# Two banks instead of one for the value products of every attention phase

## The chip, the cores and the metric

The kernel runs on one core of a Trainium2 chip. The metric is the time of one execution in device microseconds; lower is better. The engines are named as in the profile: PE (matmuls), PEld (its weight loads), DVE (VectorE), ACT (ScalarE), POOL (GpSimd) and SP (the queue that issues DMAs). A bank is one of the eight 128 x 512 fp32 areas of PSUM, into which PE writes.

## The reference: what is computed

For 2048 tokens of width 512 the kernel mixes an attention block and a token-mixing MLP by a gate per token:

```python
q, k, v = (x @ wqkv) in 32 heads of width 16
p = softmax(q k^T * 16 ** -0.5)
a = (p v) @ wo
u = gelu(layernorm(x)^T @ w1 + b1); b = (u @ w2 + b2)^T
out = g * a + (1 - g) * b          # g = sigmoid(sum(x * gate_w))
```

All of it is float32. The softmax needs exp of 32 x 2048 x 2048 scores, which is what the long middle part of the kernel does.

## The kernel before, in words

**The stages.** Up to about 284 us the kernel projects v, k and half of q and runs the first MLP layer. Then come 128 *phases* of attention, p = 0 to 127, that end near 1231 us, and last the output projection's second half. Dense work (the second MLP layer, the other half of q, the first half of the output projection) is laid beside the attention, a few matmuls with each score matmul. The change touches the phases alone.

**A phase.** 32 groups of four phases (p = 4 * grp + ph) each treat two heads and half of the queries. In a phase PE makes 16 *units* of scores, n = 0 to 15, each a 128 x 512 bank (L1067); most units have a dense matmul beside them (L1076) on the other 64 rows of the array. The work is in an order written out by hand, and every engine runs its instructions in program order.

- Units 1, 3, 5, 9, 14 and 15 (`EVAC`) are copied from their bank to SBUF by DVE (L1089), and ACT then takes exp of all six in one instruction of 3072 columns (L1102), here called the *long exp*.
- Units 0, 2, 4, 6, 7 and 8 (`SINGLE`) go through exp on ACT one by one (L1093); units 10 with 11 and 12 with 13 go in pairs (L1031).
- Then PE makes the *value products* (L963), exp(scores) times v and a column of ones. In a phase these are 12 products of the units *held* from the phase before (1 with 3, 5 with 9, 14 with 15: their long exp has run since) and 20 of the phase's own units, the *turns* (0 with 2, 4 with 6, 7 with 8 and the two pairs). In the trace each product is two matmul records: 24 and 40 records.
- DVE adds the bank of products to the group's sum `ot` in SBUF (L985). Its next instruction is the copy of unit 1 of the next phase.

Two kinds of phases matter below. With **14** dense matmuls beside the units (second MLP layer), all own turn products are of one half of the sum's columns, and PE ends the units in the order 14, 15. With **12** (`late_query`, phases p = 8m + 6 and 8m + 7 for m = 0 to 7; output projection, p = 112 to 127) units 12 to 15 mix the two heads, so the turns cover one half of the columns and 64 rows of the other half, and PE ends with 15, 14.

**The banks.** Seven banks are dealt out anew in each phase by `shares`: unit n < 7 writes bank `share[n]`, units 7 to 13 write `share[0]` to `share[6]` again, unit 14 `share[0]` and unit 15 `share[2]`. `av`, the bank of the products, is `share[1]`, which unit 8 leaves. The bank that holds the last products is given to `shares` as `spare` and is used last in the next phase, by unit 6. In ph = 0 the held units belong to the group before, so there the held products go to `av` and the turns to a second bank, `share[3]`, which unit 10 leaves; DVE then adds twice. In the other three phases of a group held products and turns add up in `av`, and DVE adds all 512 columns once:

```python
if ph == 0:
    if held:
        apply_v(av, grp - 1, held, final=True)
        spare = share[3]
        av = twos[spare]
    apply_v(av, grp, turns)
elif p < LAST:
    apply_v(av, grp, held + turns, await_loads=ph == PHASES - 1)
```

`apply_v` issues the products and then the adds. It makes one add of 128 x 512 if all four pairs of head and query half are met, and else one of 128 x 256 for each head whose two query halves are met and one of 64 x 256 for a lone one. Between the copies of units 14 and 15 and these adds DVE runs what else is due in the phase: a tiny memset `mark` (L1111), splits of weights (L67, with POOL doing L68), results of the dense work (L542, L616 to L630, L816) and steps of the output projection (L755, L756, L1119).

Of the kernel before, what the change touches and what calls it, by code (L numbers as in the profile page):

```python
# [60 lines left out]
def gated_mix(ctx: ExitStack, tc: tile.TileContext, a_x, a_wqkv, a_wo, b_w1, b_b1, b_w2, b_b2, gate_w, out):  # L61
# [116 lines left out]
    with tc.tile_pool(name="vp", bufs=1, side="right") as pool:  # L178
# [15 lines left out]
        turns = {}  # L194
# [386 lines left out]
    PHASES, NSC, BANKS = 4, 16, 7  # L581
    LAST = NG * PHASES - 1
# [220 lines left out]
    def o_matmuls(half, t, n, m):  # L803

        for i in range(n, m):
            k, j = divmod(i, 3)
            hi, lo = o_parts[half, t % 8, k]
            a, b = ((hi, wo[0]), (hi, wo[1]), (lo, wo[0]))[j]
            yield a, b[: a.shape[0], k, :]
# [114 lines left out]
    def shares(n):  # L924

        for one in range(0, BANKS, 2):
            lows = [k for k in range(one)][::2] + [k for k in range(one + 1, BANKS)][::2]
            for third in lows:
                if n in (third, third + 1):
                    first, second = (low for low in lows if low != third)  # L930
                    return [first, first + 1, one, second, second + 1, 2 * third + 1 - n, n]
# [7 lines left out]
    def column_halves(x):  # L939
        x = x.rearrange("p (i m c) -> p m i c", i=2, m=2)  # L940
        return x[:, 0], x[:, 1]

    def store(g, ot):
        half, p = divmod(g, NP)
        k, p = divmod(p, 4)
        for j in range(4):
            rows, cols = slice(32 * j, 32 * j + VC), slice(j * QC, (j + 1) * QC)
            dst = o_d[half][k][2 * p * DH : 2 * (p + 1) * DH, cols].rearrange("(i r) n -> r i n", i=2)
            nc.sync.dma_start(dst, ot[rows][:DH].rearrange("r (i n) -> r i n", i=2))
            dst = r_d[half][k][None, 2 * p : 2 * (p + 1), cols]  # L950
            nc.sync.dma_start(dst, ot[rows][DH:].rearrange("r (i n) -> r i n", i=2))

    def apply_v(av, grp, pairs, final=False, await_loads=False, between=None):

        for n, pair in enumerate(pairs):
            if between and n == len(pairs) - 2:
                between()
            for i, c, qb, pt in sorted(pair, key=lambda u: u[2]):
                for h in range(2):
                    j = 2 * qb + h  # L960
                    b, r = divmod(grp % NP * 2 + i, BH)
                    v_at = (c * BH + r) * VC
                    mm = nc.tensor.matmul(  # L963
                        av[32 * j : 32 * (j + 1), i * QC : (i + 1) * QC],
                        vb[b][:, v_at : v_at + 32],
                        pt[:, h * QC : (h + 1) * QC],
                        start=n == 0,
                        stop=n == len(pairs) - 1,
                    )
                    if await_loads and n and landed:  # L970
                        tc.add_manual_dep(mm.ins, landed.pop(0).ins.name, SYNC, reason=AHEAD_OF_USE)
        ot = sums[grp]
        met = {(i, qb) for pair in pairs for i, _, qb, _ in pair}
        every, cols, rows = slice(0, P), [slice(n * QC, (n + 1) * QC) for n in range(2)], [slice(0, HALF), slice(HALF, P)]
        if grp == NG - 1 and final:
            assert len(met) == 4
            parts = list(zip(column_halves(ot), column_halves(av)))
        elif len(met) == 4:
            parts = [(ot, av)]
        else:  # L980
            at = [(every, cols[i]) for i in range(2) if {(i, 0), (i, 1)} <= met]
            at += [(rows[qb], cols[i]) for i, qb in sorted(met) if (i, 1 - qb) not in met]
            parts = [(ot[r, c], av[r, c]) for r, c in at]
        for x, y in parts:
            latest["add"] = nc.vector.tensor_tensor(x, y, x, ALU.add)  # L985
        if final and grp < NG - 1:
            store(grp, sums.pop(grp))

    engines = {getattr(mybir.EngineType, name) for name in ("PE", "Activation", "DVE", "Pool", "SP")}
    with tc.manual_schedule(engines=engines):  # L990
        held, fence, turn, spare = [], None, 0, 0
        landed.clear()

        for p in range(LAST + 1):
            grp, ph = divmod(p, PHASES)
# [42 lines left out]
            share = shares(spare)  # L1038
# [3 lines left out]
            for n in in_turn:  # L1042
# [7 lines left out]
                else:  # L1050
                    if n == TWO[0][0]:
# [4 lines left out]
                        for low in range(BANKS):  # L1056
                            if low == share[1]:
                                av = psum.tile([P, NB], F32, name="av")
# [61 lines left out]

            turns, now_held = ([tuple(units[n] for n in pair) for pair in pairs] for pairs in (TURNS, HELD))
            spare = share[1]
            if ph == 0:
                if held:
                    apply_v(av, grp - 1, held, final=True)
                    spare = share[3]
                    av = twos[spare]
                apply_v(av, grp, turns)
            elif p < LAST:
                apply_v(av, grp, held + turns, await_loads=ph == PHASES - 1)  # L1130
            else:
                ot = sums[grp]
                nc.vector.tensor_scalar_max(ot, ot, least[0])
                first_out = ps_dn.tile([P, D], F32, name="dn")

                def meanwhile():
                    for i, (a, b) in enumerate(o_matmuls(1, NH, 0, 3)):
                        nc.tensor.matmul(first_out, a, b, start=i == 0, stop=False)

                apply_v(av, grp, held + turns + now_held, final=True, between=meanwhile)  # L1140
                last_ot = ot
            pool.__exit__(None, None, None)
            held = now_held
# [86 lines left out]
    with tc.If(far_off != 0):  # L1230
        with (
# [6 lines left out]
            for b in range(ND):  # L1238
                with tc.For_i(0, P // DH, 1) as hi:
# [11 lines left out]
                    for t in range(NS):  # L1251
# [7 lines left out]
                        p = pool.tile([P, S], F32, name="p", bufs=1)  # L1259
# [51 lines left out]
```

## Time and profile before

| what | value |
|---|---|
| median of 3 runs | 1265.47 us (1265.09 to 1265.52) |
| the profiled execution | 1265.31 us |
| its span, first to last instruction | 1263.5 us |
| mean granted TensorE clock | 0.999 |
| busy: PE, ACT, DVE, POOL | 1254.8, 1069.0, 856.7, 198.6 us |
| one phase, from end to end of the long exp | 7.41 us |

A row of a timeline gives the start in the span, the time from the first start to the last end of equal neighbours, the engine, the line, the operation, output <- inputs, the shapes and the count; in brackets stands how long the engine was idle before, and what ended that. Instructions of one engine can overlap in such rows, since the next one starts before the one before has written its last element. A row of groups gives the busy time, the mean duration in ns of one, and the idle time before.

### The profile page before, as it was taken

How to read it: one execution, taken by the hardware profiler on the slowest of the kernel's cores; microseconds unless marked ns; L12 is line 12 of the kernel's file. 1: busy time of each engine (PE TensorE's matmuls, PEld its weight loads, DVE VectorE, ACT ScalarE, POOL GpSimd, SP SyncE). 2: the span in 40 equal slices, each digit the busy share in tenths (PEclk: the TensorE clock that was granted, in tenths of full speed). 3: DMA queues.
4: the chain of work that ended last, by engine and by line, in shares of the span. 5: the costliest groups of instructions: out<-in, count | busy, mean ns of one | idle time of the engine just before them, and what ended most of it. 6: DMA issues, size and time to landing. Idle time of an engine off the chain costs nothing.

```text
span 1263.5 us, 32833 instructions
## 1 busy us (share of the span) xinstructions
PE 1254.8 (99%) x13342; PEld 829.2 (66%) x13342; DVE 856.7 (68%) x1562; ACT 1069.0 (85%) x1405; POOL 198.6 (16%) x316
## 2 busy tenths in 40 slices
PE   9999999999999999999999999999999999999998
PEld 7888888875666666666666666666666666666656
DVE  5675453178767676767677677776777677678883
ACT  4443343269999999999999999999999999999990
POOL 0220444461010101010110101111111111000000
PEclk9999999999999999999999999999999999999999
DMA  4799443244744444544344433444543443366611
GB/s 134 251 340 329 143 122 106 81 127 110 214 121 104 90 102 85 158 86 97 77 105 94 99 90 83 91 87 81 113 101 73 90 100 60 56 166 175 151 60 70
DMA packets 100556, 152.32 MB, mean 121 GB/s; under 512 B 17109, under 2 KB 56171, under 8 KB 96300
## 3 DMA queue, kind: packets, MB, share of 16 engines
q1 hardware_dynamic: 99820, 149.08, 46.0%
q8 instruction: 107, 1.75, 0.6%
q10 hardware_dynamic: 576, 1.05, 0.2%
q14 instruction: 53, 0.43, 0.1%
HBM read 105.39 MB, written 44.68 MB: 119 GB/s over the span
## 4 chain that ended last, share of the span: by engine, by line
PE 96%; DVE 2%; ACT 1%; issue 0%; DVEq 0%
PE av L963 31%; PE s L1067 21%; PE acc L424 12%; PE t L1067 9%; PE acc L75 8%; PE t L963 5%; PE dn L1076 3%; PE u L1067 3%; PE pa L1162 2%; DVE pe L1089 1%; PE acc L199 1%; PE acc L268 0%; DVE ot L985 0%; PE acc L245 0%; ACT p L1093 0%; ACT pe L1102 0%
## 5 line engine op out<-in xcount | busy, mean ns | idle before, releaser
L1093 ACT ACTIVATE p<-s 128x512 f32<-128x512 f32 x768 | 411.9, 789 | 0.1
L1102 ACT ACTIVATE pe<-pe 128x3072 f32<-128x3072 f32 x129 | 380.9, 2954 | 0.0
L1067 PE MATMUL s<-qs,ks 64*128 64x512 f32 x1280 | 329.8, 400 | 0.6 <-ACT p L1093 0.6
L1089 DVE COPY pe<-s 128x512 f32<-128x512 f32 x512 | 323.6, 685 | 5.5 <-PE s L1067 1.5
L1067 PEld LDWEIGHTS s<-qs,ks 64*128 64x128 f32 x1280 | 225.7, 184 | 92.7 <-issue 52.3
L1031 ACT ACTIVATE p<-t 128x1024 f32<-128x1024 f32 x256 | 278.7, 1267 | 0.0
L963 PE MATMUL av<-p,v 128*32 128x256 f32 x3880 | 227.2, 379 | 0.0
L1089 DVE COPY pe<-u 128x512 f32<-128x512 f32 x256 | 164.8, 685 | 67.1 <-PE u L1067 67.1
L963 PE MATMUL av<-pe,v 128*32 128x256 f32 x3072 | 192.5, 383 | 0.0
L985 DVE TENSOR_TENSOR ot<-av,ot 128x512 f32<-128x512 f32 (+2 forms) x160 | 93.0, 582 | 140.9 <-PE av L963 139.6
L68 POOL TENSOR_TENSOR w_lo<-w_raw,w_hi 128x512 fp32r<-128x512 f32 (+1 forms) x128 | 153.0, 1202 | 196.8 <-ACT w_hi L67 99.9
L1076 PE MATMUL dn<-u_lo,w_hi 64*128 64x512 f32 x448 | 181.0, 404 | 0.0
L1076 PE MATMUL dn<-u_hi,w_hi 64*128 64x512 f32 x448 | 180.7, 403 | 0.0
L963 PEld LDWEIGHTS av<-p,v 128*32 128x32 f32 x3880 | 126.0, 110 | 83.3 <-ACT p L1093 0.2
L1076 PE MATMUL dn<-u_hi,w_lo 64*128 64x512 f32 x448 | 180.6, 403 | 0.0
L1067 PE MATMUL t<-qs,ks 64*128 64x512 f32 x512 | 142.5, 413 | 0.0
L963 PEld LDWEIGHTS av<-pe,v 128*32 128x32 f32 x3072 | 86.8, 109 | 80.7 <-ACT p L1093 35.7
L1080 POOL MEMSET token<- 1x1 f32 x128 | 11.3, 88 | 742.7 <-PE dn L1076 679.4
L67 ACT CAST w_hi<-w_raw 128x512 fp32r<-128x512 f32 (+1 forms) x67 | 38.0, 569 | 82.7 <-PE acc L424 63.1
L1067 PEld LDWEIGHTS t<-qs,ks 64*128 64x128 f32 x512 | 73.2, 184 | 50.8 <-ACT p L1093 48.6
L424 PE MATMUL acc<-h_hi,w_hi 128*128 128x512 f32 x224 | 87.9, 392 | 0.0
L424 PE MATMUL acc<-h_hi,w_lo 128*128 128x512 f32 x224 | 87.9, 392 | 0.0
(171 smaller groups left out, 1615.8 us busy)
## 6 DMA issues: line engine op xcount, KB each, us to landing
w_raw<-in_B_w_dram SPq DMA_DIRECT2D x96, 256.0 KB
ks<-kp SPq DMA_DIRECT2D x192, 128.0 KB
qs<-qp SPq DMA_DIRECT2D x256, 64.0 KB
kp<-pc SPq DMA_DIRECT2D x16, 512.0 KB
qp<-pc SPq DMA_DIRECT2D x8, 768.0 KB
qp<-row SPq DMA_DIRECT2D x24, 256.0 KB
v<-v SPq DMA_DIRECT2D x4, 1088.0 KB
x<-in_A_x_dram SPq DMA_DIRECT2D x16, 256.0 KB
```

Source lines behind the costliest of these rows:

```text
L67: copy(hi, src)
L68: return sub(lo, src, hi.bitcast(F32), ALU.subtract)
L75: nc.tensor.matmul(ps, a, b, start=start and n == 0, stop=stop and n == last)
L424: nc.tensor.matmul(p, a, b, start=first and k == 0, stop=last and k == 2)
L963: mm = nc.tensor.matmul(av[32 * j : 32 * (j + 1), i * QC : (i + 1) * QC], vb[b][:, v_at : v_at + 32], pt[:, h * QC : (h + 1) * QC], start= ...
L985: latest["add"] = nc.vector.tensor_tensor(x, y, x, ALU.add)
L1031: pairs_done.append(nc.scalar.activation(pt, twos[low, low + 1], AF.Exp, scale=SCALE))
L1067: nc.tensor.matmul(s, kt[grp][rows_i, c * P : (c + 1) * P], qt[grp][rows_i, qb * NB : (qb + 1) * NB], start=True, stop=True,)
L1076: mm = nc.tensor.matmul(ps, a[half], b[half], start=begin and not second, stop=last and bool(second))
L1089: nc.vector.tensor_copy(pt, s)
L1093: one = nc.scalar.activation(pt, s, AF.Exp, scale=SCALE)
L1102: done = nc.scalar.activation(x, x, AF.Exp, scale=SCALE)
```

## The change

In every phase except the last the held products now go to `av`, with adds of their own, and the turns to a second bank, which is now `share[0]` (unit 14 leaves it) and no longer `share[3]`, in ph = 0 too. Nothing else is edited.

```diff
-            if ph == 0:
+            if p < LAST:
                 if held:
-                    apply_v(av, grp - 1, held, final=True)
-                    spare = share[3]
+                    apply_v(av, grp - (ph == 0), held, final=ph == 0)
+                    spare = share[0]
                     av = twos[spare]
-                apply_v(av, grp, turns)
-            elif p < LAST:
-                apply_v(av, grp, held + turns, await_loads=ph == PHASES - 1)
+                apply_v(av, grp, turns, await_loads=ph == PHASES - 1)
```

On DVE, in a phase of 14 dense matmuls near the start of the attention (p = 1), `u_2800` being the new bank of the turns, the end of the phase and the start of the next read so before (-) and now (+):

```order
-L985 TENSOR_TENSOR ot<-av,ot 128x512
+L985 TENSOR_TENSOR ot<-av,ot 128x256
+L985 TENSOR_TENSOR ot<-av,ot 64x256
+L985 TENSOR_TENSOR ot<-u_2800,ot 128x256
```

One add has become three, of which the last alone needs the end of the products.

On DVE in a phase of 12 dense matmuls (p = 115, output projection), from the copies of units 15 and 14 to the copy of unit 1 of the next phase, before:

```order
L1089 COPY pe<-u_16963 128x512
L1089 COPY pe<-u_16964 128x512
L816 SCALAR_TENSOR_TENSOR row<-dn,g,row 128x512
L1111 MEMSET mark 1x1
L1119 TENSOR_TENSOR o_sum<-e_16664,o_sum 128x512
L1119 CAST e_16664<-o_sum 128x512
L1119 TENSOR_TENSOR e_16664<-o_sum,e_16664 128x512
L985 TENSOR_TENSOR ot<-av,ot 128x512
L1089 COPY pe<-s_17052 128x512
```

and now, where `u_17154` is the bank that unit 14 left:

```order
L1089 COPY pe<-u_17153 128x512
L1089 COPY pe<-u_17154 128x512
L816 SCALAR_TENSOR_TENSOR row<-dn,g,row 128x512
L1111 MEMSET mark 1x1
L1119 TENSOR_TENSOR o_sum<-e_16848,o_sum 128x512
L1119 CAST e_16848<-o_sum 128x512
L1119 TENSOR_TENSOR e_16848<-o_sum,e_16848 128x512
L985 TENSOR_TENSOR ot<-av,ot 128x256
L985 TENSOR_TENSOR ot<-av,ot 64x256
L985 TENSOR_TENSOR ot<-u_17154,ot 128x256
L985 TENSOR_TENSOR ot<-u_17154,ot 64x256
L1089 COPY pe<-s_17245 128x512
```

One add has become four, two of them after the end of the products, and the copy of unit 1 stands behind all four.

On PE, at the same kind of place (p = 117), the semaphores awaited in brackets, before:

```order
L1067 MATMUL u_17227<-qs_2583,ks_2582 128x512 [waits Activation_49]
L963 MATMUL av<-pe,v_114 32x256 [waits Activation_49]
L963 MATMUL av<-pe,v_114 32x256 x11
L963 MATMUL av<-p_17185,v_114 32x256 x2
L963 MATMUL av<-p_17192,v_114 32x256 x2
```

and now:

```order
L1067 MATMUL u_17420<-qs_2583,ks_2582 128x512 [waits Activation_49]
L963 MATMUL av<-pe,v_114 32x256 [waits Activation_49]
L963 MATMUL av<-pe,v_114 32x256 x11
L963 MATMUL u_17420<-p_17378,v_114 32x256 [waits DVE_49]
L963 MATMUL u_17420<-p_17378,v_114 32x256
L963 MATMUL u_17420<-p_17385,v_114 32x256 x2
```

The products and their order are the same, but the first product of the turns now waits for DVE, which has to copy unit 14 out of the bank first.

## The prediction

> **What bounds the kernel now.** I began with the page's first part, whose busy shares mislead here.
>
> ```profile
> span 1263.5 us, 32833 instructions
> PE 1254.8 (99%) x13342; PEld 829.2 (66%) x13342; DVE 856.7 (68%) x1562; ACT 1069.0 (85%) x1405; POOL 198.6 (16%) x316
> ```
>
> PE looks full and ACT looks free for 15% of the span. The groups by shape say otherwise:
>
> ```profile
> L1093 ACT ACTIVATE p<-s 128x512 f32<-128x512 f32 x768 | 411.9, 789 | 0.1
> L1102 ACT ACTIVATE pe<-pe 128x3072 f32<-128x3072 f32 x127 | 377.9, 2976 | 0.0
> L1031 ACT ACTIVATE p<-t 128x1024 f32<-128x1024 f32 x256 | 278.7, 1267 | 0.0
> ```
>
> Before its exps, the whole work of the phases, ACT idles 0.1 us in all; its free 15% lie outside the attention. How tight it runs, the timeline of ACT in two ordinary phases shows (p = 56 and 57):
>
> ```profile
> 699.24 3.00 ACT L1102 ACTIVATE pe<-pe 128x3072 f32<-128x3072 f32 x1
> 701.94 3.24 ACT L1093 ACTIVATE p<-s 128x512 f32<-128x512 f32 x6
> 704.81 2.19 ACT L1031 ACTIVATE p<-t 128x1024 f32<-128x1024 f32 x2
> 706.65 3.00 ACT L1102 ACTIVATE pe<-pe 128x3072 f32<-128x3072 f32 x1
> ```
>
> The ends are 702.24, 705.18, 707.00 and 709.65. They follow each other with no hole, 2.94 + 1.82 + 2.65 = 7.41 us per phase, and the starts lie before the ends of the instruction ahead. So ACT is saturated and has a little queue of begun work. How large it is, a place shows where ACT had to wait (p = 116 and 117):
>
> ```profile
> 1144.56 2.86 ACT L1102 ACTIVATE pe<-pe 128x3072 f32<-128x3072 f32 x1
> 1147.23 3.12 ACT L1093 ACTIVATE p<-s 128x512 f32<-128x512 f32 x6
> ...
> 1152.22 2.77 ACT L1102 ACTIVATE pe<-pe 128x3072 f32<-128x3072 f32 x1
> 1154.89 3.02 ACT L1093 ACTIVATE p<-s 128x512 f32<-128x512 f32 x6
> ```
>
> After the wait six single exps take 3.02 us instead of 3.24: about **0.22 us** of queue had been used up. From end to end of the long exp this phase took 1154.99 - 1147.42 = 7.57, so 0.15 or 0.16 us was lost. The kernel is bound by ACT. An edit on DVE cannot make a phase shorter than 7.41 us; it can only make ACT wait.
>
> **Is DVE's last add on the path?** The split form exists already, in ph = 0. Here are p = 56 (split) and p = 57 (one add):
>
> ```profile
> 701.60 0.42 DVE L985 TENSOR_TENSOR ot<-t,ot 128x256 f32<-128x256 f32 x1 [1.04 <-issue]
> 701.74 0.40 PE L1067 MATMUL s<-qs,ks 64*128 64x512 f32 x1
> 702.17 2.52 DVE L1089 COPY pe<-s 128x512 f32<-128x512 f32 x4 [0.15 <-PE dn L1076]
> ...
> 708.82 0.50 PE L1067 MATMUL s<-qs,ks 64*128 64x512 f32 x1
> 708.96 0.69 DVE L985 TENSOR_TENSOR ot<-av,ot 128x512 f32<-128x512 f32 x1 [1.85 <-PE av L963]
> 709.16 0.39 PE L1067 MATMUL s<-qs,ks 64*128 64x512 f32 x1
> 709.59 2.52 DVE L1089 COPY pe<-s 128x512 f32<-128x512 f32 x4
> ```
>
> Unit 1 is the matmul at 701.74 and at 709.16 (708.82 is unit 0). It ends at 702.14 and at 709.55, and its copy starts 0.03 and 0.04 us later, in both forms. The shorter add leaves DVE idle for 0.15 us and gains nothing. That settles the phases with 14 dense matmuls.
>
> **The change, part by part.** Prices of the adds, from the groups:
>
> ```profile
> L985 DVE TENSOR_TENSOR ot<-av,ot 128x512 f32<-128x512 f32 x95 | 65.6, 690 | 134.4 <-PE av L963 134.1
> L985 DVE TENSOR_TENSOR ot<-av,ot 128x256 f32<-128x256 f32 x34 | 14.2, 421 | 5.5 <-PE av L963 5.5
> L985 DVE TENSOR_TENSOR ot<-av,ot 64x256 f32<-64x256 f32 x31 | 13.3, 428 | 1.0
> ```
>
> The 95 adds of 512 columns are the 95 phases that change their form. 68 of them have 14 dense matmuls and get 421 + 428 + 421 ns for 690, 27 (16 late-query, 11 output projection) get a further 428. That is 68 x 0.58 + 27 x 1.01 = 67 us more of DVE, on an engine with 134.4 us of idle time just before these adds. What counts is where it falls. Back to back such adds are about 0.45 us apart, so a pair holds DVE for 0.90 us.
>
> *1. The 68 phases with 14 dense matmuls: 0, but for four.* The held pair needs 0.90 us of DVE's wait for the products (1.85 us above), and the last add is shorter by 0.2. Where there was no idle time before the add, the next copy comes 0.90 - 0.20 = 0.7 us late. There are four such places, p = 3, 83, 89 and 101; the first, the third and the last:
>
> ```profile
> 308.38 0.69 DVE L985 TENSOR_TENSOR ot<-av,ot 128x512 f32<-128x512 f32 x1
> ...
> 944.47 1.80 DVE L1119 TENSOR_TENSOR row<-v,row 128x512 f32<-128x512 f32 x1
> 946.40 0.69 DVE L985 TENSOR_TENSOR ot<-av,ot 128x512 f32<-128x512 f32 x1
> ...
> 1035.42 0.69 DVE L985 TENSOR_TENSOR ot<-av,ot 128x512 f32<-128x512 f32 x1
> ```
>
> No row of an add shows idle time in brackets. In p = 89 (the rows at 944.47 and 946.40) the add follows 946.40 - 946.27 = 0.13 us behind other work, and I take the same for p = 101, so there the copy comes 0.57 us late, and in p = 3 and 83, with nothing between, 0.7. ACT's queue takes 0.22, and about 0.1 is slack between copy and exp (see 2): 0.3 us each, **+1.2 us**.
>
> *2. The output projection, p = 113 to 126.* Here "half of the columns" does not hold: the turns need two adds after the last product. The form is in the trace already, in ph = 0 (p = 116):
>
> ```profile
> 1128.42 1.29 DVE L1089 COPY pe<-u 128x512 f32<-128x512 f32 x2 [0.59 <-PE u L1067]
> ...
> 1131.65 0.55 DVE L756 RECIPROCAL inv<-inv 128x64 f32<-128x64 f32 x1
> ...
> 1146.86 0.86 DVE L985 TENSOR_TENSOR ot<-t,ot 128x256 f32<-128x256 f32 x2 [0.99 <-issue]
> 1147.76 2.48 DVE L1089 COPY pe<-s 128x512 f32<-128x512 f32 x4
> 1150.83 1.29 DVE L1089 COPY pe<-u 128x512 f32<-128x512 f32 x2 [0.59 <-PE u L1067]
> ...
> 1153.29 0.69 DVE L1119 TENSOR_TENSOR e<-o_sum,e 128x512 fp32r<-128x512 f32 x1
> ```
>
> ```profile
> 1144.39 2.34 PE L963 MATMUL t<-p,v 128*32 128x256 f32 x40
> ...
> 1146.67 0.49 PE L1067 MATMUL s<-qs,ks 64*128 64x512 f32 x1
> ...
> 1152.05 2.34 PE L963 MATMUL av<-p,v 128*32 128x256 f32 x40
> ```
>
> Unit 0 starts at 1146.67, and unit 1 is copied 1.09 us later, where it is 709.59 - 708.82 = 0.77 in an ordinary phase: 0.32 late. That is the wait that cost ACT 0.16 with 0.10 of queue left (3.12 - 3.02), so some 0.06 to 0.1 is slack on the way. In ph = 0 it comes once in four phases and ACT recovers; now every phase has it. And a second thing closes the circle: the turns' first product waits until DVE has copied unit 14, the last copy. From copy to copy a phase is now: four copies and units 15 and 14 with theirs, 1147.76 to 1152.12, 4.36; PE's start after a copy, some 0.06; the 40 records to unit 0, 2.28; to the first add 0.19; the pair, 0.90. Together 7.79, **0.37** over ACT's 7.42. This is the floor, in p = 113, 116, 120 and 124.
>
> Where DVE has much else to do, its own row of work is longer: 4.36, then the other work D, then both pairs, 1.80. In p = 114 D reaches from 1129.71 to 1132.20 (2.4 after overlap), in p = 117 from 1152.12 to 1153.98, 1.86. So 8.57 and 8.02, **1.15** and **0.60** over. By the timeline p = 114, 115, 118 and 122 are of the first kind, p = 117, 119, 121, 123, 125 and 126 of the second. Sum: 4 x 0.37 + 4 x 1.15 + 6 x 0.60 = 9.7; about 0.5 of that is lost already (after the four ph = 0 phases, at about the 0.16 seen here or less). **+9.2 us.**
>
> *3. The eight pairs of late-query phases.* After p = 8m + 6 there are two adds, 0.90 for 0.63, and the turns start some 0.06 later: 0.33 late. In the next phase (p = 63, before):
>
> ```profile
> 746.66 2.52 DVE L1089 COPY pe<-s 128x512 f32<-128x512 f32 x4
> ...
> 749.78 1.29 DVE L1089 COPY pe<-u 128x512 f32<-128x512 f32 x2
> ...
> 752.24 0.68 DVE L623 TENSOR_REDUCE z<-dn 128x1 f32<-128x512 f32 x1
> ```
>
> From 746.66 DVE works to 752.92 and then has 1.80 us of adds: 8.06 from copy to copy, 0.64 over. Of 0.97 in all, 0.22 goes into ACT's queue and 0.1 into slack: 0.65 per pair, **+5.2 us**, and six ordinary phases lie between pairs for the queue to fill again.
>
> **The sum.** 1.2 + 9.2 + 5.2 = 15.6 us on the profiled execution's 1265.3 (span 1263.5 and 1.8 around it; the median of 1265.47 is the same within 0.2): **1280.9 us**.
>
> No row shows PE's own wait for the copy of unit 14. Its price lies between 0, if the 12 held products take as long as the copies, and 0.2 us, about half a matmul's 0.40, in each of 27 phases; I took 0.06 after the copies' end. They end at 1152.12 and the turns began at 1152.05, so the wait itself moves PE by 0.13.
>
> **Rivals.**
>
> *The held adds are held up by POOL* (slower still). In 16 phases POOL splits two weights, some 2 us right when the held adds are due. If these had to wait for POOL, they would end about 0.7 us later: 16 x 0.4 = 6.5 more, 1287. POOL's row at the place above:
>
> ```profile
> 944.43 2.43 POOL L68 TENSOR_TENSOR w_lo<-w_raw,w_hi 128x512 fp32r<-128x512 f32 x2 [1.76 <-DVE w_hi L67]
> ```
>
> The DVE product of two SBUF tiles at 944.47 took 1.80 us beside it, but the add of `av` at 946.40 took its usual 0.69 although POOL was at work until 946.86. So I give this 6%. The Trainium skill ("SBUF — State Buffer", "Who interferes with whom") says that a DVE instruction with two SBUF inputs contends with a GpSimd instruction that reads SBUF, and one with at most one SBUF input outside the two-port modes does not; these adds read `av` from PSUM, so by that rule the 6.5 us would not come, and the rows agree.
>
> *Not slower: ACT's queue takes it all.* One mechanism, at ACT's wait for the copies of units 14 and 15: a lateness under 0.22 us, with quiet phases after it in which the queue fills, costs nothing. For it: the 0.32 us in p = 117 cost only 0.16. It decides if the second add costs DVE little (the one add of 512 columns took 0.69, the pair 0.86 and a start); if each late phase stayed under that point, 2 and 3 would shrink to their full-DVE phases' queue and the time be 1265 to 1268. Against it: the pair comes 0.32 late where it can be seen, and from p = 113 no quiet phase follows. 7%.
>
> *Faster: the last add was what the next phase waited for.* Then each of the 68 phases would gain what DVE now idles after the short add, 0.15 us: 10.2 us, and with nothing of 1 to 3 the time would be 1255. It needs unit 1's copy to start late in the one-add form, and it starts 0.04 us after unit 1; and ACT's ends leave no hole. 3%.
>
> *Milder: only the phases whose DVE is full pay.* If the loop of 7.79 ran at 7.5 in fact, 1280.9 less 4 x 0.3 in 2 and less 8 x 0.3 in 3, and 0.2 less in each longer phase: 1275. This belongs to the forecast's range.
>
> **Numbers.** The forecast with its milder form has 84%, the rivals 6, 7 and 3. Range 1272 to 1288: from a loss of 6.7 us, where the copies' slack is twice what I took and the DVE-full phases overlap more, to POOL's rival. A measurement of this kernel can tell about 0.2%, 2.5 us, from no change. Faster by more 0.03, within 0.06, slower 0.91.
>
> **What would show it.** In the profile after: ACT's long exps still 7.41 us apart in phases of 14 dense matmuls; two more idle stretches on ACT after each late-query pair, some 0.65 us together; 7.8 to 8.6 us per phase from p = 113; DVE's adds of 64x256 more numerous than 150; PE's units 15 and 14 waiting for DVE copies. The forecast is wrong if late phases stay at 7.4, or if ordinary ones move.

## The result and the profile after

| | before | changed |
|---|---|---|
| median of 3 runs | 1265.47 us | 1276.86 us (1276.43 to 1278.03) |
| ratio | | 1.009, interval 1.0077 to 1.0104 |
| profiled execution, its span | 1265.31, 1263.5 us | 1276.43, 1274.7 us |
| from the end of the first to that of the last long exp | 936.15 us | 947.01 us |

The change made the kernel 11.4 us slower; 15.4 had been forecast, within a range that reaches from 6.5 to 22.5 over before. The long exps hold 10.86 us of it. What lies ahead of the first long exp, 0.36 us here, is chance, since up to there the two programs are the same: in the kernels below that exp ends anywhere from 285.5 to 286.3 us. Behind the last long exp the change shows once more, since the end of p = 126 is late too. ACT's first work after the attention, before and now:

```profile
1234.69 0.41 ACT L1180 CAST e<-o_sum 128x256 fp32r<-128x256 f32 x1 [5.24 <-DVE o_sum L1179]
```

```profile
1246.59 0.41 ACT L1178 CAST e<-o_sum 128x256 fp32r<-128x256 f32 x1 [5.77 <-DVE o_sum L1177]
```

This cast starts 12.74 us after the end of the last long exp before and 13.41 us now, 0.67 us later. How much of that reaches the end of the program these runs can't tell, since the last stage, from ACT's last ACTIVATE on, takes anywhere from 21.1 to 22.4 us in the profiled executions of all the kernels here.

The page's first part and the groups of ACT and DVE by shape:

```profile
PE 1265.5 (99%) x13342; PEld 836.1 (66%) x13342; DVE 918.4 (72%) x1779; ACT 1076.1 (84%) x1405; POOL 198.8 (16%) x316
```

```profile
L1102 ACT ACTIVATE pe<-pe 128x3072 f32<-128x3072 f32 x127 | 368.3, 2900 | 2.1 <-DVE pe L1089 1.0 <-DVE mark L1111 0.3
...
L985 DVE TENSOR_TENSOR ot<-av,ot 128x256 f32<-128x256 f32 x129 | 53.6, 416 | 10.7 <-PE av L963 10.7
L985 DVE TENSOR_TENSOR ot<-av,ot 64x256 f32<-64x256 f32 x126 | 53.5, 425 | 2.0
L985 DVE TENSOR_TENSOR ot<-u,ot 128x256 f32<-128x256 f32 x126 | 53.5, 425 | 105.0 <-PE u L963 101.7 <-PE s L1067 0.5
```

DVE works 62 us more. ACT's long exps now have idle time ahead of them, 2.1 us, of which the row puts 1.3 down to DVE; before there was none. That is less than the loss: the rest shows in shorter records (a mean of 2900 ns for 2976), since with the queue empty an exp no longer starts under the end of the one ahead.

Three places of the changed kernel show how it went. First, an ordinary phase of 14 dense matmuls, the end of p = 57 and the start of p = 58 (the kernel before has one add in this phase), on PE and on DVE:

```profile
712.66 0.50 PE L1067 MATMUL s<-qs,ks 64*128 64x512 f32 x1
...
713.00 0.40 PE L1067 MATMUL s<-qs,ks 64*128 64x512 f32 x1
```

```profile
710.83 0.86 DVE L985 TENSOR_TENSOR ot<-av,ot 128x256 f32<-128x256 f32 x2
712.79 0.42 DVE L985 TENSOR_TENSOR ot<-u,ot 128x256 f32<-128x256 f32 x1 [1.10 <-PE u L963]
713.43 2.55 DVE L1089 COPY pe<-s 128x512 f32<-128x512 f32 x4 [0.22 <-PE dn L1076]
```

The held pair stands in time that DVE had free, the last add ends at 713.21, and DVE waits 0.22 us for unit 1, whose matmul ends at 713.40. The copy starts 0.03 us after it, as before.

Second, ACT's long exps from p = 113 on:

```profile
1127.10 2.77 ACT L1102 ACTIVATE pe<-pe 128x3072 f32<-128x3072 f32 x1
1134.66 2.77 ACT L1102 ACTIVATE pe<-pe 128x3072 f32<-128x3072 f32 x1
1143.24 2.77 ACT L1102 ACTIVATE pe<-pe 128x3072 f32<-128x3072 f32 x1 [0.35 <-DVE pe L1089]
1151.60 2.77 ACT L1102 ACTIVATE pe<-pe 128x3072 f32<-128x3072 f32 x1 [0.30 <-DVE mark L1111]
1159.34 2.77 ACT L1102 ACTIVATE pe<-pe 128x3072 f32<-128x3072 f32 x1
1166.97 2.77 ACT L1102 ACTIVATE pe<-pe 128x3072 f32<-128x3072 f32 x1
```

All have the 2.77 us of an empty queue, and the starts follow each other by 7.56, 8.58, 8.36, 7.74 and 7.63 us where 7.42 is ACT's own work. Third, DVE in p = 117 and at the end of p = 118:

```profile
1157.96 1.29 DVE L1089 COPY pe<-u 128x512 f32<-128x512 f32 x2 [0.58 <-PE u L1067]
1159.28 0.75 DVE L816 SCALAR_TENSOR_TENSOR row<-dn,g,row 128x512 f32<-128x512 f32 x1
...
1161.02 0.74 DVE L985 TENSOR_TENSOR ot<-av,ot 128x256 f32<-128x256 f32 x2
1161.86 0.75 DVE L985 TENSOR_TENSOR ot<-u,ot 128x256 f32<-128x256 f32 x2
1162.53 1.87 DVE L1089 COPY pe<-s 128x512 f32<-128x512 f32 x3
```

```profile
1169.19 0.86 DVE L985 TENSOR_TENSOR ot<-av,ot 128x256 f32<-128x256 f32 x2
...
1170.15 0.87 DVE L985 TENSOR_TENSOR ot<-u,ot 128x256 f32<-128x256 f32 x2
1171.05 0.69 DVE L1089 COPY pe<-s 128x512 f32<-128x512 f32 x1
```

The same four adds take 1.51 us in p = 117 (1161.02 to the copy at 1162.53) and 1.86 in p = 118. This difference, which the forecast didn't know of, is the subject of two experiments.

### The profile page after: what moved, and what is told of

Read it like the earlier page. It is cut to its first block, busy times and chain, and to the rows that moved or that the text cites. A ratio compares the mean times of both kernels' runs of the same rounds, so it can differ in the third digit from the quotient of the medians.

```text
span 1274.7 us, 33314 instructions
## 1 busy us (share of the span) xinstructions
PE 1265.5 (99%) x13342; PEld 836.1 (66%) x13342; DVE 918.4 (72%) x1779; ACT 1076.1 (84%) x1405; POOL 198.8 (16%) x316
## 4 chain that ended last, share of the span: by engine, by line
PE 97%; DVE 1%; ACT 1%; DMA 0%; issue 0%; SPq 0%; DVEq 0%
PE s L1067 22%; PE u L963 21%; PE av L963 15%; PE acc L424 12%; PE t L1067 9%; PE acc L75 8%; PE dn L1076 4%; PE u L1067 3%; PE pa L1160 2%; PE acc L199 1%; DVE pe L1089 0%; PE acc L268 0%; DMA x<-in_A_x_dram 0%; DVE ot L985 0%; ACT p L1093 0%; ACT pe L1102 0%
## 5 line engine op out<-in xcount | busy, mean ns | idle before, releaser
L1093 ACT ACTIVATE p<-s 128x512 f32<-128x512 f32 x768 | 403.7, 717 | 2.0 <-PE dn L1076 1.4
L1102 ACT ACTIVATE pe<-pe 128x3072 f32<-128x3072 f32 x129 | 371.2, 2878 | 2.1 <-DVE pe L1089 1.0
L963 PE MATMUL u<-p,v 128*32 128x256 f32 x5040 | 295.8, 380 | 0.0
L1031 ACT ACTIVATE p<-t 128x1024 f32<-128x1024 f32 x256 | 268.7, 1189 | 0.0
L963 PEld LDWEIGHTS u<-p,v 128*32 128x32 f32 x5040 | 160.7, 110 | 115.5 <-DVE pe L1089 11.1
L985 DVE TENSOR_TENSOR ot<-u,ot 128x256 f32<-128x256 f32 (+1 forms) x157 | 65.2, 423 | 105.2 <-PE u L963 101.7
L985 DVE TENSOR_TENSOR ot<-av,ot 64x256 f32<-64x256 f32 (+1 forms) x255 | 105.9, 421 | 12.7 <-PE av L963 10.7
```

The source lines that it names most:

```text
L963: mm = nc.tensor.matmul(av[32 * j : 32 * (j + 1), i * QC : (i + 1) * QC], vb[b][:, v_at : v_at + 32], pt[:, h * QC : (h + 1) * QC], start= ...
L1031: pairs_done.append(nc.scalar.activation(pt, twos[low, low + 1], AF.Exp, scale=SCALE))
L1093: one = nc.scalar.activation(pt, s, AF.Exp, scale=SCALE)
L1102: done = nc.scalar.activation(x, x, AF.Exp, scale=SCALE)
```

## The experiments

Loss is read below as the distance from one long exp's end to the next, less the kernel before's (start plus duration, from rows like those above). "Places" are the four phases of 14 dense matmuls where DVE is full, "pairs" the eight late-query pairs (both with the phase after them, in which the rest of the lateness comes out), "full" the four projection phases 115, 116, 119 and 123 (the lateness arises in the phase before), "after ph = 0" the phases 113, 117, 121 and 125, "others" the remaining six from 114 to 126.

| kernel | median us | ratio and interval | places | pairs | full | after ph = 0 | others | sum |
|---|---|---|---|---|---|---|---|---|
| changed | 1276.86 | 1.009 [1.0077, 1.0104] | 0.76 | 3.50 | 4.40 | 0.64 | 1.55 | 10.86 |
| only 14 dense matmuls | 1265.49 | 1.0001 [0.9991, 1.001] | 0.79 | 0.0 | 0.0 | -0.12 | 0.04 | 0.75 |
| only 12 | 1275.63 | 1.0077 [1.006, 1.0094] | 0.0 | 3.46 | 4.39 | 0.63 | 1.57 | 10.03 |
| only the projection | 1272.05 | 1.0053 [1.0038, 1.0068] | 0.0 | 0.0 | 4.38 | 0.65 | 1.58 | 6.55 |
| turns in share[3] | 1277.68 | 1.0096 [1.0079, 1.0113] | 1.93 | 3.37 | 4.87 | 0.31 | 1.58 | 12.13 |
| that, held bank to unit 4 | 1276.99 | 1.0089 [1.0072, 1.0106] | 0.90 | 3.38 | 4.86 | 0.31 | 1.58 | 11.15 |
| rows dealt anew | 1272.15 | 1.0053 [1.0036, 1.007] | 0.33 | 1.84 | 3.65 | -0.05 | 1.34 | 7.15 |
| before, rows dealt anew | 1265.04 | 0.9996 [0.9987, 1.0005] | 0.0 | 0.0 | 0.0 | -0.44 | 0.09 | -0.38 |
| unit 13 to held bank, first | 1275.67 | 1.0081 [1.0065, 1.0096] | 0.81 | 5.68 | 2.24 | 0.64 | 1.13 | 10.46 |
| unit 13 to held bank, third | 1269.98 | 1.0034 [1.0021, 1.0046] | 0.80 | 0.20 | 2.21 | 0.57 | 0.96 | 4.80 |
| that, rows dealt anew | 1268.11 | 1.0019 [1.0009, 1.0028] | 0.35 | 0.21 | 1.88 | -0.08 | 0.82 | 3.37 |
| held adds left out | 1270.33 | 1.0039 [1.0024, 1.0055] | 0.76 | 1.97 | 1.07 | 0.57 | 0.86 | 5.22 |
| all mends | 1267.30 | 1.0014 [1.0004, 1.0024] | 0.48 | 0.0 | 1.71 | -0.45 | 0.04 | 2.73 |

The sum is of all distances up to the last long exp, in one profiled execution of each kernel. The medians also hold the stages ahead of the first long exp and behind the last, which vary by a microsecond, so the two can differ by about as much. In the last kernel 0.94 us of the sum lies in none of the columns, 0.74 of that in p = 71 of this one execution, where DVE waits 1.82 us for a load of `wo`; elsewhere this remainder is under 0.2.

### Which phases pay

The first three kernels make the change in some phases only. `parted` is the condition, here for the first of them (`n_b` is the number of dense matmuls in the phase, `NSC` is 16); in the second kernel it is `n_b < NSC - 2`, in the third `p >= 112`:

```diff
+            parted = n_b == NSC - 2
-            if p < LAST:
+            if ph == 0 or parted and p < LAST:
                 if held:
                     apply_v(av, grp - (ph == 0), held, final=ph == 0)
-                    spare = share[0]
+                    spare = share[0 if parted else 3]
                     av = twos[spare]
                 apply_v(av, grp, turns, await_loads=ph == PHASES - 1)
+            elif p < LAST:
+                apply_v(av, grp, held + turns, await_loads=ph == PHASES - 1)
```

> Two banks only in the phases of 14 dense matmuls; the 27 phases of 12 keep the one add. My theory: these phases gain and lose nothing but at the four full places, which measured 0.26 + 0.19 + 0.16 + 0.15 = 0.76 us in the changed kernel, so 1266.2 us, and the long exps of all other phases stay 7.41 to 7.42 us apart. Rival, the form costs something in each of its phases, hidden in the 7.42: some 3 us or more, 1268 to 1269. Rival, the shorter last add is a gain that the other phases' loss covers: below 1264.

Measured: 1265.49 us, 1.0001 with an interval of 0.9991 to 1.001. The four places lose 0.27, 0.19, 0.17 and 0.16 us by the long exps, together what they lose in the changed kernel, and no other phase lost anything. So the 68 phases neither gain nor hide a cost; a loss of 0.8 us is less than these runs can show.

> Two banks (and the bank that unit 14 leaves) only in the 27 phases of 12 dense matmuls, the old form elsewhere. My theory: nearly all of the loss stays, 3.5 us in the eight late-query pairs and 6.6 in the output projection by the distances of the long exps in the changed kernel: 1265.5 + 10.1 = 1275.6 us. Rival, that the loss needs the other 68 phases as well (ACT's queue never full when the pairs come): clearly under 1274.

Measured: 1275.63 us. The loss comes without the other 68 phases.

> Two banks only in the output projection (p = 112 and later); the old form in the late-query pairs and the 68 other phases. My theory: the two kinds of places add up independently, 1265.5 + 6.6 = 1272.1 us, with the distances of the long exps as in the changed kernel from p = 113. Rival, the projection's loss builds on lateness brought along from earlier phases: the first late phases come out at 7.42 and the sum under 1271.

Measured: 1272.05 us, and every distance from p = 113 on is that of the changed kernel within 0.03 us. The parts add up.

### PE's wait for the copy of unit 14

PE in the changed kernel, in an ordinary phase (p = 5) and in p = 117:

```profile
320.25 1.50 PE L963 MATMUL av<-pe,v 128*32 128x256 f32 x24
321.57 2.34 PE L963 MATMUL u<-p,v 128*32 128x256 f32 x40
323.84 0.49 PE L1067 MATMUL s<-qs,ks 64*128 64x512 f32 x1
```

```profile
1157.86 1.50 PE L963 MATMUL av<-pe,v 128*32 128x256 f32 x24
1159.30 2.37 PE L963 MATMUL u<-p,v 128*32 128x256 f32 x40
1161.60 0.50 PE L1067 MATMUL s<-qs,ks 64*128 64x512 f32 x1
```

From the first held product to unit 0 these are 3.59 and 3.74 us: the wait is worth 0.15 us of PE where it exists (order 15, 14). The turns begin 1.44 us after the held products where it was 1.32, so most of it is the wait itself, the 0.13 us that the forecast read from the rows; the rest is that the turns then take 0.03 us longer. To take it away, the turns went to the old second bank:

```diff
-                    spare = share[0]
+                    spare = share[3]
```

> The changed kernel, but the turns go to share[3], which unit 10 leaves, so that their first product doesn't wait for DVE's copy of unit 14. My theory: the wait costs PE about 0.05 us per late phase (the 24 records of held products begin at 1150.115 us and follow each other by 0.058, the turns begin at 1151.563, where they could at 1151.51), so 0.5 us in all: 1276.3 us, and the phases of the output projection that took 7.70 take 7.65. Rival, the wait for the copy is what closes the circle from copy to copy: then the phases at 7.70 return to 7.42 and the pairs lose half, about 1272 us.

Measured: 1277.68 us, against both theories, and by the long exps 1.3 us slower than with the wait (the runs alone overlap: 1277.44 to 1278.10 against 1276.43 to 1278.03). PE's products took 3.59 us again, but the end of PE's wait brought nothing: among the others, from p = 120 on, the distances rose from 7.69 to 7.71 to 7.73 to 7.74 us, since DVE's row of work decides there. In p = 117, 121 and 125 they fell from 7.74 or 7.75 to 7.65. And something new was lost where DVE is full, 0.3 us in each place and 0.38 in p = 116. PE and DVE of this run at the end of p = 3:

```profile
308.05 0.50 PE L1067 MATMUL s<-qs,ks 64*128 64x512 f32 x1
309.09 0.47 PE L1067 MATMUL s<-qs,ks 64*128 64x512 f32 x1 [0.54 <-DVE ot L985]
```

```profile
308.10 0.85 DVE L985 TENSOR_TENSOR ot<-av,ot 128x256 f32<-128x256 f32 x2
309.08 0.43 DVE L985 TENSOR_TENSOR ot<-t,ot 128x256 f32<-128x256 f32 x1
```

The second row is unit 1 of the next phase. It waits until the held adds end at 308.95, because it is to write the bank that they read: `shares` deals the banks by the spare one, and with this spare the held products' bank goes to unit 1; with `share[0]` it goes to unit 5, which comes later. In PE's waits by the profile L985 has 4.5 us in 8 such places here, 1.2 us in 4 with the changed kernel. To test that, the same kernel with the banks dealt the other way round:

```diff
-    def shares(n):
+    def shares(n, last=None):
...
                     first, second = (low for low in lows if low != third)
+                    if last in (first, first + 1):
+                        first, second = second, first
...
-            share = shares(spare)
+            share = shares(spare, share[1] if p else None)
```

> The changed kernel with the turns in share[3], as in the run that came out slower, but the banks of the next phase are dealt out so that the held products' bank goes to its unit 4 and not to its unit 1 (in the changed kernel it goes to unit 5). My theory, that run was slower because unit 1 of the next phase had to wait for the held adds where DVE is full (at 309.09 us it started 0.15 us after the end of the held adds): the four places with 14 dense matmuls return from 7.86 to 7.98 to 7.53 to 7.64, p = 116 from 8.74 to about 8.36, and with the 0.155 us of PE's wait gone the sum comes to 1275.8 us, 1 us under the changed kernel. Rival, the last add itself is late since its bank was read by ACT before: it stays at 1277.7 us.

Measured: 1276.99 us, not the 1275.8 expected; by the long exps it lies between the two. The four places came back to 7.66, 7.57, 7.57 and 7.55 us, as my theory had it. But p = 116 stayed at 8.74, where 8.36 was expected. PE and DVE at the end of p = 115:

```profile
1144.65 0.49 PE L1069 MATMUL s<-qs,ks 64*128 64x512 f32 x1
```

```profile
1144.95 0.74 DVE L987 TENSOR_TENSOR ot<-av,ot 128x256 f32<-128x256 f32 x2
1146.18 0.75 DVE L987 TENSOR_TENSOR ot<-t,ot 128x256 f32<-128x256 f32 x2 [0.49 <-PE dn L1078]
1146.85 1.27 DVE L1091 COPY pe<-s 128x512 f32<-128x512 f32 x2
```

Unit 0 starts at 1144.65, so the turns had ended, and still their first add waits 0.49 us after the held pair; at 309.08 in the run before, this distance was 309.08 - 308.95 = 0.13. The run before has the same wait at this place (0.48 us), so it goes with `share[3]` and not with the dealing; less the 0.10 us of the changed kernel at this place (1146.39 to 1146.49) it is the 0.38 us lost there. What is awaited in this one phase is open.

### The rows of an add of 64 rows

In p = 117 of the changed kernel all four adds begin at row 0; in p = 118 both adds of 64 rows take rows 64 to 127, and so it goes in all odd and even phases of the projection. Which half it is comes from `turn`, which deals the halves of the queries to the units that mix the heads. In a new dealing the turns' lone rows are always 0 to 63:

```diff
             n_b = len(beside)
+            turn = 1 - second
```

> The changed kernel with the halves of the queries dealt out so that in phases of 12 dense matmuls the turns' lone add of 64 rows is always on rows 0 to 63, and the held ones' on rows 64 to 127. In the changed kernel the next DVE instruction starts 0.08 us before the end of an add when both begin at row 0, and 0.01 to 0.03 us after it when one begins at row 64: pairs of adds take 0.67 us in odd phases and 0.90 in even ones. My theory, it is the rows: all last pairs take 0.67 and all held pairs 0.88, even phases of the projection shorten by up to 0.2 and odd ones lengthen by about 0.1, 1276.0 to 1276.6 us in all. Rival, it is the bank or the half of the columns: the spacings stay as they are by phase parity, 1276.9 us.

Measured: 1272.15 us, ratio 1.0053 with an interval of 1.0036 to 1.007: 4.7 us under the changed kernel by the medians, 3.7 by the long exps, several times what was expected. DVE in p = 116 and 117:

```profile
1150.97 0.75 DVE L985 TENSOR_TENSOR ot<-u,ot 128x256 f32<-128x256 f32 x2 [1.08 <-PE u L963]
1151.64 2.52 DVE L1090 COPY pe<-s 128x512 f32<-128x512 f32 x4
1154.74 1.29 DVE L1090 COPY pe<-u 128x512 f32<-128x512 f32 x2 [0.59 <-PE u L1068]
1155.95 0.74 DVE L816 SCALAR_TENSOR_TENSOR row<-dn,g,row 128x512 f32<-128x512 f32 x1
...
1157.68 0.86 DVE L985 TENSOR_TENSOR ot<-av,ot 128x256 f32<-128x256 f32 x2
1158.64 0.75 DVE L985 TENSOR_TENSOR ot<-u,ot 128x256 f32<-128x256 f32 x2
```

The last pair of p = 116 now takes 0.67 us (1150.97 to 1151.64); in the changed kernel it was 0.89 there, and 0.90 in p = 118 (1170.15 to 1171.05). The bank and the half of the columns are as they were, so it is the rows. What I had wrong was the other side: the odd phases didn't get longer. Their held pair does cost 0.12 us more (1157.68 to 1158.64, where it was 1161.02 to 1161.86), but L816 begins 0.08 us before the end of the copies at 1156.03, where in the changed kernel it begins 0.03 us after their end at 1159.25. In the changed kernel itself the first instruction behind the copies also begins 0.03 us after their end in p = 115 and 117 and 0.08 us before it in p = 116 and 118, whose forerunners end with adds at row 0. So an add at row 64 is paid for once more, later, by the next instruction that reads SBUF.

The same line in the kernel before touches only the two last adds of the ph = 0 phases:

> The kernel before with the same new dealing of query halves: its two last adds in the ph = 0 phases of the projection then begin at row 0. My theory: those pairs take 0.67 us for 0.90, and ACT's losses after p = 112, 116, 120 and 124 (0.06 to 0.15 us each, 0.43 in all) go: 1265.0 us, as much under the kernel before as the runs can just show, and 7.42 to 7.44 us for p = 113, 117, 121 and 125. Rival, the losses are PE's: 1265.5 us and 7.48 to 7.57 as before.

Measured: 1265.04 us, ratio 0.9996 with an interval of 0.9987 to 1.0005. ACT's long exps of p = 116 and 117:

```profile
1144.38 3.00 ACT L1103 ACTIVATE pe<-pe 128x3072 f32<-128x3072 f32 x1
1151.83 2.97 ACT L1103 ACTIVATE pe<-pe 128x3072 f32<-128x3072 f32 x1
```

The last pair now takes 0.67 us (from 1146.73 to the copy at 1147.40), the long exps end 7.42 apart, and so do those of p = 113, 121 and 125 (7.48, 7.53 and 7.55 before). That is all that ACT had left to give in these phases: 0.4 us, which the profile shows and the runs can't tell from nothing. It is the only kernel here whose sum is below that of the kernel before.

### The second add at the end, and the total of DVE's work

First, unit 13's products (the lone 64 rows of the turns) go to the held bank, where that half is added anyhow; ahead of the other turns, in one list with the held products (the rest of this edit, which lets a bank's two halves of rows begin and end their sums apart, is left out here):

```diff
+                    if ph and n_b < NSC - 2:
+                        lone = next(u for u in turns[-1] if u[0] != second)
+                        turns[-1] = tuple(u for u in turns[-1] if u[0] == second)
+                        held = held + [(lone,)]
                     apply_v(av, grp - (ph == 0), held, final=ph == 0)
```

> The changed kernel, but in phases of 12 dense matmuls with ph of 1 to 3 unit 13's two products (the turns' lone 64 rows of the other half) go to the held products' bank, where that half is added anyhow. So one add of 128x256 is left after the last product, and DVE does three adds for four. My theory, the loss is the pair of adds at the end and, where DVE is full, the total of adds: the projection's phases at 7.70 return to 7.42 to 7.45 except after ph = 0, the four full ones drop by 0.33 to 0.45 each to about 8.15, the pairs lose at most 0.1: 0.8 + 3.1 + 0.5 + 0.4 over before, 1270.3 us. Rival, it is PE's wait for the copy of unit 14 and not the adds: no phase but the full ones changes, 1275 us or more.

Measured: 1275.67 us, a miss. The projection went the way of my theory, though the others stopped short of 7.45 (full phases 7.91 to 8.03, others mostly 7.54 to 7.59, for 7.70), and the pairs got worse, 7.76 and 7.79 us. PE in p = 7:

```profile
335.13 1.50 PE L968 MATMUL av<-pe,v 128*32 128x256 f32 x24
336.82 0.41 PE L968 MATMUL av<-p,v 128*32 128x256 f32 x2 [0.18 <-ACT p L1036]
...
339.14 0.49 PE L1072 MATMUL s<-qs,ks 64*128 64x512 f32 x1
```

The held products would be through 1.32 us after 335.13, at 336.45, yet unit 13's begin at 336.82: they wait for ACT, which reads the last pair of units late. Where ACT is full, a product of that pair can't come first without such a wait. In the next kernel this pair is third in the turns, and unit 13's products stay beside unit 12's (the bank chosen per unit in a function for held products and turns together):

```diff
+        todo = [[(av, unit) for unit in pair] for pair in held]
+        todo += [[(av if unit[0] != second else u, unit) for unit in pair] for pair in turns[:2] + turns[4:] + turns[2:4]]
```

> As the run that sent unit 13's products to the held bank, but they stay beside unit 12's in one pass of PE, and this pair of units comes third in the turns. There unit 13 alone had taken a pass of its own, and the value products took 3.78 to 4.13 us (3.59 in the kernel before, 3.745 in the changed one). My theory, that this pass and the early need of the last pair's exp ate the gain: the products take 3.745 us again, the late-query pairs lose at most 0.1, the projection's phases at 7.70 come under 7.50, the full ones stay near 8.0 and those after ph = 0 near 7.74: 0.8 + 2.2 + 0.9 + 0.2 + 0.4 over before, 1270.0 us. Rival, PE's wait of 0.155 us for the copy of unit 14 is enough by itself to keep the loop over 7.42: the projection's phases stay at 7.54 to 7.58 and the pairs lose 0.3, 1272 us or more.

Measured: 1269.98 us, ratio 1.0034 with an interval of 1.0021 to 1.0046. The seven later pairs lose nothing any more (7.41 to 7.44 us), the full phases take 7.91 to 8.02, those after ph = 0 in p = 117, 121 and 125 7.72 to 7.75; the others stay at 7.54 to 7.57 from p = 120 on, not under 7.50. The extra pass of PE that I named isn't borne out: from 336.82 to unit 0 at 339.14 the turns took 2.32 us in the run before, and 2.30 in the changed kernel (1159.30 to 1161.60). What the pairs lost was the wait for ACT. And the rival was half right: PE's wait for the copy does keep the others over 7.42, as the last kernel below shows by leaving it out, though not the pairs.

Then both this and the rows:

```diff
+            turn = 1 - second if n_b == NSC - 2 or ph == 0 else second
```

> The run before this one with the query halves dealt out so that nearly all adds of 64 rows lie on rows 0 to 63 (all of ph = 0's last ones, and the held ones but those of the phases after ph = 0). My theory, both savings add: the phases after ph = 0 drop from 7.74 to 7.55, the four full ones and the four full places with 14 dense matmuls by about 0.1 each: 1.5 us less than without, 1268.5 us. Rival, rows matter only for the last adds: 0.6 us less.

Measured: 1268.11 us, ratio 1.0019 with an interval of 1.0009 to 1.0028, as my theory had it: 1.4 us less by the long exps, 1.9 by the medians. The phases after ph = 0 in p = 117, 121 and 125 fell to 7.53 to 7.56, the places by about 0.1, the full phases by 0.1 but for p = 116.

The other way to take work from DVE is to leave the held adds out:

```diff
-        for x, y in parts:
+        for x, y in parts[:0] if drop else parts:
...
-                    apply_v(av, grp - (ph == 0), held, final=ph == 0)
+                    apply_v(av, grp - (ph == 0), held, final=ph == 0, drop=ph != 0 and n_b < NSC - 2)
```

> The changed kernel without the adds of the held products in phases of 12 dense matmuls with ph of 1 to 3 (those products are left out of the sum). My theory: the four full phases at 8.36 to 8.61 us pay for the total of DVE's work and drop by the whole pair, to about 7.7; the others, which pay for the last pair only, stay at 7.64 to 7.75; the second phase of each late-query pair loses about 0.2 less. 0.8 + 1.2 + 2.1 + 1.6 over before, 1271.2 us. Rival, the full phases are long because the held adds come between the end of the products and the last adds through a wait of theirs for PE, not by their work: they stay over 8.2.

Measured: 1270.33 us, ratio 1.0039 with an interval of 1.0024 to 1.0055. The full phases came down to 7.75, 7.54, 7.74 and 7.72 us. DVE at the end of p = 115:

```profile
1142.36 0.69 DVE L1119 TENSOR_TENSOR e<-o_sum,e 128x512 fp32r<-128x512 f32 x1
1142.96 0.74 DVE L985 TENSOR_TENSOR ot<-u,ot 128x256 f32<-128x256 f32 x2
1143.63 2.47 DVE L1089 COPY pe<-s 128x512 f32<-128x512 f32 x4
```

The last pair follows DVE's other work with no idle time even now: in these phases it is DVE's total that counts, as expected. The others but p = 114 fell too, to between 7.54 and 7.57, which I had not expected: in the changed kernel their held pair stands right behind other work as well (at 1161.02 in p = 117, after an instruction of 0.69 us that starts at 1160.41), and without it the last pair no longer waits.

Last, all mends together: turns in `share[3]` with the held bank going to unit 4, unit 13 in the held bank, and the rows.

> All mends of the two-bank form together: turns in share[3] with the held bank going to unit 4, unit 13's products in the held bank beside unit 12's, adds of 64 rows on rows 0 to 63. My theory: what is left is DVE's total work in the four full phases of the projection (some 0.45 us each) and the four full places before (0.1 each): 1265.5 + 1.8 + 0.5 = 1267.8 us; all other phases 7.41 to 7.45. It can't come under the kernel before, since ACT is full there. Rival, that the two-bank form has a gain of its own once its costs are gone: under 1265.0 us.

Measured: 1267.30 us, ratio 1.0014 with an interval of 1.0004 to 1.0024. From p = 113 on all phases but the full ones take 7.40 to 7.43 us, and so do the pairs: with one add left at the end, PE's wait for the copy gone does pay, 0.82 to 0.04 us in the others. The full ones take 7.69, 7.95, 7.82 and 7.92. The remainder is DVE's work where DVE has no room. No gain of the two-bank form shows: with the rows alone dealt anew the kernel before takes 1265.04 us.

## Why the prediction was right, and where its sizes were off

| term | predicted | measured |
|---|---|---|
| 1. 64 ordinary phases of 14 dense matmuls | 0 | 0.0 |
| 1. four full places of them | 1.2 | 0.76 |
| 2. projection, four full phases | 4.6 | 4.40 |
| 2. projection, p = 113, 116, 120 and 124 | 1.0 | 0.76 |
| 2. projection, second kind, p = 117 to 126 | 3.6 | 2.07 |
| 3. eight late-query pairs | 5.2 | 3.50 |
| sum | 15.6 | 11.5 |

The terms go by the phases of the forecast, whose lateness shows in the next long exp (p = 113 in that of p = 114, which stands among the others above). That of p = 126, 0.67 us of the second kind, shows in the cast behind the last one. The medians are 11.4 us apart.

**The bound, right.** ACT is full, and an edit on DVE could only make it wait. The ordinary phases stayed as they were (0.01 us in all), and the most that any of these kernels gained from ACT's waits in a stage was 0.45 us.

**Step 1, right.** Unit 1's copy starts 0.03 us behind unit 1 in the new form too, and the kernel with the change in these phases alone takes the time of before. The four places are those that were named; they cost 0.15 to 0.26 us instead of 0.3.

**The price of a pair of adds, too high.** This is the step that failed in size: "back to back such adds are about 0.45 us apart, so a pair holds DVE for 0.90 us". The row for it came from p = 116, a phase with ph = 0, and the kernel before has such last pairs only there, at rows 64 to 127. In odd phases they lie on rows 0 to 63 and take 0.67 us. So four adds hold DVE for 1.51 us there, not 1.80, and this alone takes the second kind of phases, which I had at 8.02 us, down to 7.73, where 7.63 to 7.71 was measured. With 1.80 for p = 118 the four full phases, three of which come from even phases, were sized well.

**Step 3, right in its mechanism.** DVE in the first pair, p = 6 and 7, at the first copy of each phase:

```profile
324.60 2.53 DVE L1089 COPY pe<-s 128x512 f32<-128x512 f32 x4 [0.20 <-PE s L1067]
...
332.38 2.48 DVE L1089 COPY pe<-s 128x512 f32<-128x512 f32 x4
...
338.65 0.42 DVE L985 TENSOR_TENSOR ot<-av,ot 128x256 f32<-128x256 f32 x1
...
339.50 0.75 DVE L985 TENSOR_TENSOR ot<-u,ot 128x256 f32<-128x256 f32 x2
340.17 1.27 DVE L1089 COPY pe<-s 128x512 f32<-128x512 f32 x2
```

From copy to copy these are 7.78 and 7.79 us, 0.37 late each, 0.74 together, where 0.33 and 0.64, together 0.97, was forecast; the four adds of p = 7, an odd phase, take 1.52 us and not 1.80, which is the difference. The later pairs are as late (7.77 to 7.79 us) and lost 0.41 to 0.44 us. So ACT's queue and the slack on the way took 0.32, what the forecast gave them; in the first pair, which follows soon after the first place, they took only 0.2.

**The floor of the projection, nearly.** 7.79 us was forecast for the circle from copy to copy; p = 116, 120 and 124 took 7.72 or 7.73, and p = 113, an odd phase with the shorter last pair, 7.53. The wait for the copy of unit 14, whose price was unknown between 0 and 0.2 us, is 0.15 us. It is on PE's way but not on DVE's, and taking it away gained little as long as two adds stood at the end.

**The rivals.** POOL didn't hold up the held adds: apart from the four places, no phase of 14 dense matmuls moved, and where POOL splits weights beside them these adds take 0.41 and 0.43 us on average, for 0.42 and 0.43 without it. By the Trainium skill's page "SBUF — State Buffer", section "Who interferes with whom", it should not, and the trace agrees. ACT's queue took the first 0.32 us of a pair and nothing from p = 113 on, where no quiet phase follows. The faster case needed a late copy of unit 1 in the old form, and there was none. What the forecast called milder, 1275 us, comes nearest to the measurement in number, by luck and not by its mechanism: the loop did not run at 7.5 us, and phases whose DVE is not full paid too. What was less is the price of the adds in odd phases.

## What to carry to other kernels

Splitting one instruction to get part of it off the end pays only where the end waits for that instruction; look first at whether the next one on the engine starts as soon as its own input is there. Price the split by the phases in which the engine is full, since there each added instruction counts in full, and take the price of an instruction from the same shape at the same rows, not from the nearest name. A bank freed earlier or later is not free either: see which unit is dealt that bank next, and on whom it then waits.

## What the runs showed of the hardware that was not expected

An add of 256 columns costs DVE 0.33 to 0.34 us to the next instruction's start if both begin at row 0, and 0.43 to 0.46 if one of them begins at row 64. Over all adds of the changed kernel, where nothing else is awaited, the next instruction starts 0.07 to 0.09 us before the end of an add in the first case, and 0.01 to 0.03 us after it in the second. The next reader of SBUF pays 0.11 us once more even after six copies from PSUM (L816, above).

The Trainium skill ("VectorE: DVE Perf Modes", "Two Vector instructions with no wait between them") has the rule, as a model: an instruction waits for all earlier ones to finish if an input starts in another group of 32 partitions than the last read of that memory, or its output in another than the last write. The runs agree, the late payment by L816 included. The price here is about 0.1 us for each instruction so held: some 0.2 us for a pair of adds, and 3.7 us of the long exps (4.7 us of the median) for the changed kernel.
